# A transformer block on one core: a new ScalarE formula in the build's clock, fillers of zeros into open sums, earlier due times for side work

## The chip, the core and the metric

The kernel runs on one core of a Trainium2 chip. The core has a matrix engine (PE, with its weight loads shown apart as PEld), VectorE (DVE), ScalarE (ACT), GpSimd (POOL) and a queue that issues transfers (SP). The metric is device time in microseconds of one execution; times before are three runs, a profile is one execution of its own.

## The reference

One block with conditioning: a normalization scaled and shifted by vectors made from `c`, attention with 32 heads of 16, a residual, a second such normalization, a gated feed-forward network (FFN), a residual.

```python
h = _layernorm(x) * (1 + ca) + sa
x = x + ga * (softmax(q @ k.T * 16 ** -0.5) @ v) @ wo        # 2048 tokens, D = 512, H = 32
h = _layernorm(x) * (1 + cb) + sb
x = x + gb * ((gelu(h @ w_gate) * (h @ w_up)) @ w_down)      # F = 1792
```

## The kernel before

The program is written by a planner. `_Recorder` notes every instruction with what it reads and writes, works out the semaphores, and keeps a clock of its own, the build's clock: `cost` (L298 on) gives the duration of an ACT, DVE or POOL instruction, `model` the time of each engine. `probe` asks when an instruction could start. The order of instructions on each engine follows from these estimates, and the chip then runs that fixed order.

Attention runs over nine sets of query tokens: seven of 256 and two of 128 (sets 7 and 8). A unit is a set (some units take two sets together) with a group of four heads (`qd`); a round is a unit with a part of the keys; each round has four positions, and one position fills one PSUM bank of 512 scores. There are 2048 positions. Sets end at the positions 384, 512, 768, 1024, 1280, 1536, 1792, 1984 and 2048 (`ends`). The scores live in `ps_sc`, six banks in two halves of three. ScalarE takes a half with one exponential of three banks (128x1536), or of two (128x1024) where VectorE converts the third: it makes the bits of the exponential in one instruction, and after four banks (a group, "quad" in the code) three shifted copies (`shift_task`) that serve as parts of a better approximation. The products with V add into `ps_pv`, or for the second unit into the last bank of `ps_sc`; such a sum is open from the unit's first product to its last, then DVE copies it out (`unit_end`).

All other matrix work, the side work, goes through the one bank `ps_mi`: projections, output projection (`side_wo`), FFN (`side_ffn`), the transposes for it (`side_t`, `side_t2`). `plan` (L1277 on) lists it with a first position and a due position for each piece; from these comes a rate, and with every exponential the credit for side work grows by rate times positions, up to 4096. `next_side` and `advance` take the pieces in this order; while one holds the bank, `self.open` is true. In the loop of `stream` side work may run where the build's clock sees room; with a credit over 1536 it goes before the products with V. A new group for VectorE is begun, from position 1536 on, only while the credit is below CREDIT = 3500 (or where side work waits for the attention itself).

`short` sums the matmul columns of the last 3413 ns of the build's clock; below FILL = 3700 a filler may run: a product of the identity with a tile of `xs` into `ps_sc`, if the half is free but the exponential before it leaves time, or into `ps_mi`, if no piece holds it.

After the last position, `tail` finishes the sets 7 and 8: the gate and up products of set 7 that are not yet done, all those of set 8, and their down projections. Set 7's FFN can begin once its transposes (`t2T`) are done; these come in `before_last`, which takes turns with the FFN of set 6 for `ps_mi`.

Of the kernel before, what the change touches and what calls it, by code (L numbers as in the profile page):

```python
# [7 lines left out]
BF16 = mybir.dt.bfloat16  # L8
# [5 lines left out]
P = 128  # L14
# [9 lines left out]
VW = DH + 1  # L24
# [8 lines left out]
NSETS = len(SETS)  # L33
OCOL = (0, 256, 0, 256, 0, 256, 0, 256, 384)
BCOL = (0,) * (NSETS - 1) + (128,)
QJ = 4
QS = 4
MERGED = (((0, 1), (2, 3), (4, 5), (6,), (7,)), ((0, 1), (2, 3), (4,), (5,), (6,), (7,)))
CH = 3
SC = 2 * CH  # L40
# [49 lines left out]
class _Recorder:  # L90
# [21 lines left out]
    def sb(self, name, shape, dt):  # L112
        t = self.nc.alloc_sbuf_tensor(name, shape, dt)
        n = 1
        for s in shape[1:]:
            n *= s
        self.pitch[name] = n * mybir.dt.size(dt)
        self.kind[name] = "sb"
        return t
# [178 lines left out]
    def cost(self, eng, out, ins, kind):  # L298
        n = 1
        for _, k in (out if kind != "bn" else ins[0]).ap[1:]:  # L300
            n *= int(k)
        aps = [out] + list(ins)
        ps = any(self.kind.get(a.tensor.name) == "ps" for a in aps)
        small = all(mybir.dt.size(a.dtype) == 2 for a in aps)
        if eng == "act":
            return n * 0.833 + (51 if ps else 92)
        if eng == "pool":
            return n * 3.0 + 100
        f = 1
        if not ps:  # L310
            f = {("ts", True): 4, ("ts", False): 2, ("tt", True): 2}.get((kind, small), 1)
        elif small:
            f = 1.4
        return n * 1.042 / f + 68 + (95 if kind == "bn" else 0)
# [116 lines left out]
class _Kernel(_Recorder):  # L431
# [12 lines left out]
    def alloc(self):  # L444
        sb, ps = self.sb, self.ps
# [59 lines left out]
        self.rm4 = self.den[:, 0, 0:4]  # L505
        self.rm = sb("rm", [P, 2], FP32)
        self.ident = sb("ident", [P, P], BF16)
        self.ones = dreg[:, 10 * D:10 * D + P]
        self.half = dreg[:, 10 * D + P:10 * D + 2 * P]
        self.self32 = sb("self32", [P, P], FP32)  # L510
# [6 lines left out]
    def prologue(self):  # L517
        sp, act, pe, dve, pool = "sp", "act", "pe", "dve", "pool"
# [17 lines left out]

        half = self.half
        self.memset(dve, self.warm, 0.0)
        self.memset(dve, half[:, 0:2], 0.5)
        self.memset(dve, self.ones, 1.0)  # L540
        self.memset(dve, self.pv[:, :], 0.0)
# [546 lines left out]
    def side_ffn(self, gi, part=None):  # L1088

        q0, W = SETS[gi]  # L1090
        n = W // P
# [63 lines left out]
        def U(ci):  # L1155
# [4 lines left out]
            for b0 in range(0, m, kpb):  # L1160
# [5 lines left out]
                    self.task([lambda: self.tt("dve", prod[:, fcs[0]:fcs[0] + m, c0:c0 + W], w.rearrange("p (k n) -> p k n", k=m),  # L1166
                                               g.rearrange("p (k n) -> p k n", k=m), ALU.mult)], ("prod", gi, ci))
                yield END
        early = [part is not None]

        def near():
            if early[0] and ("osb", gi + 1, 5) in self.have:
                early[0] = False
                yield from self.near_end(gi + 1, 5, self.mi)
        nch = len(chunks)
# [101 lines left out]
    def plan(self, ends, nsplit, begin):  # L1277

        def at(i):
            return i * 2.5 if i < nsplit / 2.5 else nsplit + 3 * (i - nsplit / 2.5)  # L1280
        a = ends[0] + 33
        w = [(self.side_first, 0, at(30))]
        w.append((self.side_wo_load, at(30), at(30)))
        w.append((lambda: self.side_dc(1), at(30), at(51)))
        w.append((self.side_mod, at(50), at(59)))
        w.append((self.scale_wo, at(59), at(59)))
        b, c = begin[2] - 12, begin[3] - 12
        w.append((lambda: self.side_dc(2), at(59), b))
        w.append((lambda: self.side_dc(3), b, c))
        for g in range(1, 4):  # L1290
            w.append((lambda g=g: self.side_q_all(g), c + (a - c) * (g - 1) // 3, c + (a - c) * g // 3))
        n = ends[-1]
        m = NSETS - 2
        for k in range(m):
            s0 = ends[k] + 33
            e = ends[m] + 60
            if k < m - 1:
                e = max(ends[k + 1] + 30, ends[0] + 33 + (e - ends[0] - 33) * sum(SETS[k]) // SETS[m][0])
            w.append((lambda k=k: self.side_wo(k), s0, min(e, s0 + 15 * SETS[k][1] // P)))
            if k < m - 1:  # L1300
                w.append((lambda k=k: self.side_ffn(k), s0, e))
            else:
                w.append((lambda k=k: self.turns(self.before_last(m), self.side_ffn(k)), s0, e))
        k, s0 = NSETS - 2, ends[-2] - 16
        w.append((lambda: self.either(self.side_ffn(k, True), self.near_end(k + 1, 6, lambda: self.spare[2]), self.wo_last(k + 1), self.tail_rest(k, self.mi[:, :])), s0, n - 20))
        res = []
        for mk, s, e in w:
            self.dry = True
            tot = sum(y[0] for y in mk() if y is not None)
            self.dry = False  # L1310
            res.append([mk(), s, e, tot, None])
        return res
# [43 lines left out]
    def stream(self):  # L1356
# [9 lines left out]
        m = NSETS - 2  # L1366
        units = [((0, 1), qd, 0, 512) for qd in range(QJ)]
# [8 lines left out]
        ends = [0] * NSETS  # L1376
# [13 lines left out]
        for u in units[2:]:  # L1390
            n, kpb = NKT * u[3] // 512, 512 // u[3]
            plain = list(range(T0 // kpb))
            m = len(plain) * 2 // 3
# [111 lines left out]
        while cg <= group[units[-1]]:  # L1505
# [114 lines left out]
            if self.short(t) > 0 and not self.open and gap > 213 and self.probe(  # L1620
                    lambda: self.mm(self.mi[:, :], *filler)) <= t + 30:
                self.mm(self.mi[:, :], *filler)
                continue
            nxt = [x for x in [tq, ts] + [x[0] for x in tp] if x is not None and x > t + 30]
            if self.tasks:
                nxt.append(max(self.free["dve"], t + 100))
# [55 lines left out]
    def unit_end(self, u, acc):  # L1682
        sets, qd, q0, W = u
        b, lo, hi = self.osb_span(u)
        assert not self.blocked(u)
        self.copy("dve", self.osb[:, lo:hi], acc[:, 0:W])
        if sets[0] >= NSETS - 2 and len(sets) == 1 and qd >= (6 if sets[0] == NSETS - 2 else 5):
            self.done(("osb", sets[0], qd))
            return
        self.live[u] = (lo, hi)  # L1690
        two = W == 256 and sets[0] < NSETS - 2 or len(sets) > 1 and sets[0]
        if two and qd % 2 == 0:
            return
        us = [u]
        if two:
            us, lo, b = [(sets, qd - 1, q0, W), u], lo - W, b - 1
        L = hi - lo
        m = 4 * L // P
        o = 8 if BCOL[sets[0]] else 0
        sem = b + 4 * (o > 0)  # L1700
        late = EARLY if qd < 6 else (0, 0, 0)
        s2 = self.scr2[b, P * o:P * o + 4 * L]
        den, rden = self.den[:, b, o:o + m], self.rden[:, b, o:o + m]
        c = OCOL[sets[0]]
        steps = [
            ("sp", lambda: self.dma("sp", den, self.osb[DH:P:32, lo:hi].rearrange("j (a n) -> j a n", n=m), "db%d" % sem, late=late[0])),
            lambda: self.recip(rden, den),
            ("sp", lambda: self.dma("sp", s2.rearrange("(p n) -> p n", p=P), rden, "dc%d" % sem)),
            ]
        steps += [("sp", lambda j=j: self.dma(  # L1710
            "sp", self.rb[32 * j:32 * j + DH, lo:hi],
            s2[L * j:L * j + L].rearrange("(o n) -> o n", o=1).broadcast_to([DH, L]), "dd%d%d" % (sem, j), late=late[1]))
            for j in range(4)]

        def fin2():
            n = len(us)
            self.tt("dve", self.onorm[:, qd + 1 - n:qd + 1, c:c + W], self.osb[:, lo:hi].rearrange("p (a n) -> p a n", a=n),
                    self.rb[:, lo:hi].rearrange("p (a n) -> p a n", a=n), ALU.mult)
            if self.probing is None:
                for v in us:  # L1720
                    self.live.pop(v)
                for v in us:
                    for k in sets:
                        self.done(("half" if v[1] in odd else "onorm", k, v[1]))

        odd = [g[1] for g in self.merged(sets[0]) if len(g) == 2]

        def merge(j):
            self.dma("sp", self.onorm[32 * j + DH:32 * j + 2 * DH, 0:2 * len(odd):2, c:c + W], self.onorm[32 * j:32 * j + DH, 1:2 * len(odd):2, c:c + W],
                     "de%d" % j, late=late[2])  # L1730
            if self.probing is None and j == 3:
                for k in sets:
                    for x in odd:
                        self.done(("onorm", k, x))

        def free():
            return ("den", u) in self.have and all(
                ("wo", k) in self.have for k in range(sets[0]) if OCOL[k] < c + W and c < OCOL[k] + SETS[k][1])
        self.task(steps, ("den", u))
        self.task([fin2], ("norm", u), free)  # L1740
        if qd == odd[-1]:
            self.task([("sp", lambda j=j: merge(j)) for j in range(4)], None,
                      self.after([("half", k, x) for k in sets for x in odd] + [("onorm", k, x - 1) for k in sets for x in odd]))
# [220 lines left out]
```

## Time and profile before

| | us |
|---|---|
| median of three runs (827.96 to 829.52) | 828.34 |
| the profiled execution | 828.3 |
| its span, first to last instruction | 826.5 |
| mean granted clock of PE | 0.989 |

The page gives the busy time of each engine over the span. The chain of work that ended last is followed back from the last instruction to what released it. Groups are instructions of one line and form: busy time, mean duration, and idle time before them. Where instructions of an engine overlap, the mean duration of one is longer than the distance between two starts.

### The profile page before, as it was taken

How to read it: one execution, taken by the hardware profiler on the slowest of the kernel's cores; microseconds unless marked ns; L12 is line 12 of the kernel's file. 1: busy time of each engine (PE TensorE's matmuls, PEld its weight loads, DVE VectorE, ACT ScalarE, POOL GpSimd, SP SyncE). 2: the span in 40 equal slices, each digit the busy share in tenths (PEclk: the TensorE clock that was granted, in tenths of full speed). 3: DMA queues.
4: the chain of work that ended last, by engine and by line, in shares of the span. 5: the costliest groups of instructions: out<-in, count | busy, mean ns of one | idle time of the engine just before them, and what ended most of it. 6: DMA issues, size and time to landing. Idle time of an engine off the chain costs nothing.

```text
span 826.5 us, 37027 instructions
## 1 busy us (share of the span) xinstructions
PE 753.5 (91%) x17040; PEld 366.2 (44%) x17040; DVE 722.6 (87%) x1452; ACT 792.4 (96%) x746; POOL 4.5 (1%) x12
## 2 busy tenths in 40 slices
PE   8889899998989898999899989989899889988898
PEld 4333334333544444334444444344534443346557
DVE  7854878999999999999999799999988999979854
ACT  6999999999999999999999899999999999999982
POOL 2000000000000000000000000000000000000000
PEclk9989999999999999999999799999999999999999
DMA  9100000012451054103420243005423532200000
GB/s 299 53 12 13 10 9 11 10 27 59 136 146 33 16 161 121 40 10 110 125 86 16 78 130 97 25 22 164 110 68 107 178 93 66 72 10 11 18 12 13
DMA packets 94498, 57.35 MB, mean 69 GB/s; under 512 B 17030, under 2 KB 91911, under 8 KB 94343
## 3 DMA queue, kind: packets, MB, share of 16 engines
q1 hardware_dynamic: 93812, 54.47, 23.1%
q8 instruction: 133, 2.18, 1.1%
q10 hardware_dynamic: 530, 0.53, 0.2%
q14 instruction: 23, 0.18, 0.1%
HBM read 50.04 MB, written 2.35 MB: 63 GB/s over the span
## 4 chain that ended last, share of the span: by engine, by line
ACT 84%; PE 15%; DVE 1%; issue 1%
ACT E L338 81%; PE ps_sc L325 6%; PE ps_mi L325 5%; PE ps_pv L325 3%; ACT wreg L338 3%; PE ps_mi L329 0%; DVE mreg L350 0%; DVE xs L342 0%; DVE wreg L342 0%; DVE wreg L355 0%; PE ps_sc L329 0%; DVE wreg L350 0%; ACT hreg L338 0%; DVE osb L359 0%; DVE kT L359 0%
## 5 line engine op out<-in xcount | busy, mean ns | idle before, releaser
L338 ACT ACTIVATE E<-ps_sc 128x1024 bf16<-128x1024 f32 (+2 forms) x700 | 767.7, 1349 | 19.7 <-PE ps_sc L325 19.4
L325 PE MATMUL ps_sc<-qT,kT 32*128 32x256 bf16 (+3 forms) x2048 | 202.3, 275 | 26.7 <-ACT E L338 22.6
L325 PE MATMUL ps_sc<-qo,kT 32*128 32x256 bf16 (+2 forms) x2048 | 197.5, 274 | 27.1 <-ACT E L338 24.8
L325 PE MATMUL ps_pv<-E,vaug 128*17 128x256 bf16 (+2 forms) x3232 | 156.8, 275 | 1.0 <-DVE osb L359 0.7
L350 DVE TENSOR_SCALAR dreg<-ps_sc 128x512 uint16<-128x512 f32 x192 | 130.4, 685 | 13.9 <-PE ps_sc L325 13.2
L325 PE MATMUL ps_mi<-wreg,mreg 128*32 128x256 bf16 x2816 | 117.0, 277 | 4.2 <-DVE wreg L355 2.1
L325 PEld LDWEIGHTS ps_sc<-qT,kT 32*128 32x128 bf16 (+1 forms) x2048 | 62.1, 92 | 117.1 <-ACT E L338 101.9
L325 PEld LDWEIGHTS ps_sc<-qo,kT 32*128 32x128 bf16 x2048 | 59.9, 92 | 119.7 <-ACT E L338 111.6
L325 PEld LDWEIGHTS ps_pv<-E,vaug 128*17 128x17 bf16 x3232 | 60.5, 89 | 61.6 <-issue 40.8
L325 PEld LDWEIGHTS ps_mi<-wreg,mreg 128*32 128x32 bf16 x2816 | 64.7, 96 | 40.8 <-issue 25.5
L325 PE MATMUL ps_pv<-mreg,vs 128*17 128x256 bf16 (+2 forms) x1796 | 79.9, 269 | 2.1 <-issue 1.7
L350 DVE TENSOR_SCALAR mreg<-dreg 128x2048 uint16<-128x2048 uint16 x120 | 80.8, 682 | 1.0 <-PE ps_pv L325 0.8
L350 DVE TENSOR_SCALAR kq<-ps_sc 128x512 uint16<-128x512 f32 x96 | 65.2, 685 | 5.2 <-PE ps_sc L325 4.7
L350 DVE TENSOR_SCALAR mreg<-ps_sc 128x512 uint16<-128x512 f32 x96 | 65.2, 685 | 5.0 <-PE ps_sc L325 4.5
L325 PEld LDWEIGHTS ps_pv<-mreg,vs 128*17 128x17 bf16 x1796 | 40.0, 91 | 16.5 <-issue 6.5
L359 DVE CAST wreg<-ps_mi 128x512 bf16<-128x512 f32 x49 | 33.5, 684 | 5.2 <-PE ps_mi L325 4.2
L325 PE MATMUL ps_mi<-hreg,wreg 128*32 128x512 bf16 (+1 forms) x496 | 37.3, 384 | 0.5 <-DVE vaug L359 0.2
L355 DVE SCALAR_TENSOR_TENSOR wreg<-wreg,ps_mi 128x512 bf16<-128x512 bf16 x49 | 33.2, 678 | 1.9 <-ACT wreg L338 1.1
L342 DVE TENSOR_TENSOR wreg<-wreg 128x1024 bf16<-128x1024 bf16 (+1 forms) x56 | 34.3, 614 | 0.0
L350 DVE TENSOR_SCALAR mreg<-kq 128x2048 uint16<-128x2048 uint16 x48 | 32.1, 680 | 2.0 <-PE ps_pv L325 1.9
L350 DVE TENSOR_SCALAR mreg<-mreg 128x2048 uint16<-128x2048 uint16 x48 | 32.5, 677 | 0.1
L338 ACT ACTIVATE wreg<-wreg 128x1024 bf16<-128x1024 bf16 (+1 forms) x28 | 31.1, 1111 | 0.0
(171 smaller groups left out, 701.0 us busy)
## 6 DMA issues: line engine op xcount, KB each, us to landing
mreg<-in_B_w_up_dram SPq DMA_DIRECT2D x46, 256.0 KB, 3.0
mreg<-in_B_w_gate_dram SPq DMA_DIRECT2D x42, 256.0 KB, 3.1
dreg<-in_B_w_down_dram SPq DMA_DIRECT2D x18, 256.0 KB, 3.4
rb<-scr_rec SPq DMA_DIRECT2D x120, 32.0 KB, 2.3
mreg<-in_B_w_down_dram SPq DMA_DIRECT2D x12, 256.0 KB, 3.7
ereg<-in_B_w_down_dram SPq DMA_DIRECT2D x12, 256.0 KB, 3.5
mreg<-in_w_mod_dram SPq DMA_DIRECT2D x1, 2048.0 KB, 12.9
out_dram<-xs SPq DMA_DIRECT2D x15, 128.0 KB, 1.7
```

What stands on the lines that cost most here:

```text
L325: return self.rec("pe", lambda e: e.matmul(out, lhsT, rhs, start=start, stop=stop, tile_position=tp), [lhsT, rhs], [out], cost=(n, int(rhs ...
L338: return self.rec("act", lambda e: e.activation(out, in_, func, scale=scale, **kw), rd, wr, cost=self.cost("act", out, [in_], "act"))
L342: return self.rec(eng, lambda e: e.tensor_tensor(out, a, b, op), [a, b], [out], cost=self.cost(eng, out, [a, b], "tt"))
L350: return self.rec(eng, lambda e: e.tensor_scalar(out, a, s1, s2, **kw), rd, [out], cost=self.cost(eng, out, [a], "ts") + 60 * (len(rd) - 1 ...
L355: return self.rec("dve", lambda e: e.scalar_tensor_tensor(out, a, s, b, op0=op0, op1=op1), rd, [out], cost=self.cost("dve", out, [a, b], " ...
L359: return self.rec(eng, lambda e: e.tensor_copy(out, in_), [in_], [out], cost=self.cost(eng, out, [in_], "ts"))
```

## The change

```diff
+LONE = max(5, QS)
...
         if eng == "act":
-            return n * 0.833 + (51 if ps else 92)
+            return n * 0.8333 + (64 if ps else 82)
...
+        self.zero = sb("zero", [P, P], BF16)
...
         self.memset(dve, self.warm, 0.0)
+        self.memset(pool, self.zero[:, :], 0.0)
...
-        early = [part is not None]
+        early = [part is not None and LONE == 5]
...
-            if early[0] and ("osb", gi + 1, 5) in self.have:
+            if early[0] and ("osb", gi + 1, LONE) in self.have:
...
             s0 = ends[k] + 33
-            e = ends[m] + 60
+            e = ends[m] - (20)
             if k < m - 1:
                 e = max(ends[k + 1] + 30, ends[0] + 33 + (e - ends[0] - 33) * sum(SETS[k]) // SETS[m][0])
...
                 self.mm(self.mi[:, :], *filler)
                 continue
+            if self.short(t) > 0 and pos < nseq:
+                u = next((u for u in units if group[u] == cg and u in begun and left[u] > 0), None)
+                if u is not None and gap > u[3] / 2.4:
+                    def nought():
+                        for j in range(4):
+                            self.mm(acc_of(u)[32 * j:32 * j + VW, 0:u[3]], self.zero[:, 0:VW], filler[1][:, 0:u[3]], start=False, stop=False, tp=(0, 32 * j))
+                    if self.probe(nought) <= t + 30:
+                        nought()
+                        continue
...
-        if sets[0] >= NSETS - 2 and len(sets) == 1 and qd >= (6 if sets[0] == NSETS - 2 else 5):
+        if sets[0] >= NSETS - 2 and len(sets) == 1 and qd >= (6 if sets[0] == NSETS - 2 else LONE):
...
-        if two and qd % 2 == 0:
+        if two and qd % 2 == 0 and (sets, qd + 1, q0, W) in self.units:
             return
         us = [u]
-        if two:
+        if two and qd % 2:
             us, lo, b = [(sets, qd - 1, q0, W), u], lo - W, b - 1
```

Four edits act on the program. The estimate of a ScalarE instruction becomes 0.8333 ns per element plus 64 ns from PSUM (it was 0.833 and 51) or 82 ns otherwise (it was 92). A tile of zeros is set up on POOL. Where `short` calls for a filler and the older places for one did not serve, four matmuls with the zeros as stationary operand add nothing to the sum of a unit that is begun and not ended, if the next scores are further away than one such matmul takes. And the due position from which the FFN's times are worked out moves from `ends[7] + 60` = 2044 to `ends[7] - 20` = 1964. LONE has the value 5, with QS = 4.

## The prediction

> **What bounds the kernel now.** I read the page first: the span, the busy times, the chain of work that ended last, the costliest group.
>
> ```profile
> span 826.5 us, 37027 instructions
> ...
> ACT 84%; PE 15%; DVE 1%; issue 1%
> ...
> L338 ACT ACTIVATE E<-ps_sc 128x1024 bf16<-128x1024 f32 (+2 forms) x700 | 767.7, 1349 | 19.7 <-PE ps_sc L325 19.4
> ```
>
> ScalarE's exponentials set the end: 767.7 us in this one group, and 84% of the chain. So a microsecond is won where ScalarE waits, where it gets less to do, or behind its last exponential. The table by stretches says where it waits (busy time of PE, weight loads, DVE, ACT, POOL with counts, then granted clock, DMA share, GB/s).
>
> ```profile
> 43.80:47.30 3.50, 2.27 (x23) 0.89 (x23) 2.53 (x8) 3.50 (x4) 0.00 (x0) 1.00 0.01 2
> 47.30:54.20 6.90, 6.83 (x49) 2.18 (x49) 1.80 (x4) 5.57 (x6) 0.00 (x0) 0.51 0.01 2
> 453.60:457.00 3.40, 2.41 (x46) 0.89 (x42) 1.92 (x7) 3.40 (x4) 0.00 (x0) 0.99 0.00 0
> 457.00:467.10 10.10, 10.04 (x132) 3.70 (x128) 6.01 (x12) 8.39 (x8) 0.00 (x0) 0.50 0.18 52
> 467.10:505.00 37.90, 34.75 (x890) 18.52 (x886) 36.72 (x66) 37.13 (x36) 0.00 (x0) 1.00 0.45 129
> 505.00:700.00 195.00, 178.58 (x4081) 84.52 (x4083) 185.76 (x353) 195.00 (x186) 0.00 (x0) 1.00 0.33 92
> 700.00:757.00 57.00, 51.37 (x1292) 26.34 (x1289) 50.05 (x99) 57.00 (x52) 0.00 (x0) 1.00 0.12 33
> 757.00:777.00 20.00, 17.20 (x674) 12.85 (x676) 17.32 (x39) 18.94 (x17) 0.00 (x0) 1.00 0.10 17
> 800.00:826.50 26.50, 23.30 (x337) 19.57 (x325) 13.01 (x38) 7.24 (x14) 0.00 (x0) 0.98 0.05 15
> ```
>
> From 505 to 757 us ScalarE never pauses. At 47.3 and at 457.0 the granted clock falls to half for 6.9 and 10.1 us: there PE is always busy and ScalarE idles 6.90 - 5.57 = 1.33 and 10.10 - 8.39 = 1.71 us, with 37.90 - 37.13 = 0.77 us more just after. Ahead of each fall PE had little to do: 2.27 of 3.50 us and 2.41 of 3.40. And after 800, with the exponentials over, 26.5 us of tail belong to PE (23.3 busy).
>
> **The zero matmuls.** PE around the first fall and ahead of the second (start, length, operation, count, idle before):
>
> ```profile
> 45.76 0.62 PE L329 MATMUL ps_mi<-ident,dreg 128*128 128x128 bf16 x8
> 46.31 0.39 PE L325 MATMUL ps_sc<-qT,kT 32*128 32x512 bf16 x2
> 47.37 0.61 PE L325 MATMUL ps_sc<-qT,kT 32*128 32x512 bf16 x3 [0.67 <-ACT E L338]
> ```
>
> ```profile
> 454.12 0.40 PE L325 MATMUL ps_pv<-E,vaug 128*17 128x256 bf16 x8
> 455.14 0.10 PEld L325 LDWEIGHTS ps_sc<-xs,ident 128*32 128x32 bf16 x4 [0.91 <-ACT E L338]
> 455.14 0.40 PE L325 MATMUL ps_sc<-xs,ident 128*32 128x512 bf16 x4 [0.62 <-ACT E L338]
> ```
>
> Both times transposes (L329) held ps_mi open, so the old filler had no bank; PE stood 0.67 and 0.62 us. The new branch goes there: four matmuls of zeros into the open sum. A stationary operand of 17 columns over 256 moving columns takes 0.40 us in a group of 8, by the first row of the second fence, pipeline end included, so some 0.11 us for four; over 512 columns some 0.21. The branch fires only where the build's clock sees a longer gap, so the time is PE's idle time. PE's idle time in the two thin stretches, 1.23 and 0.99 us, holds five long or nine short ones at most. I take the whole of 1.33 + 1.71 + 0.77 = 3.8 us as won; the bounds are -3.8 and 0 (the clock falls as before).
>
> Do zeros count as work? The kernel's own start answers: its warm-up matmuls multiply a tile that was set to zero.
>
> ```profile
> 1.25 2.31 PE L325 MATMUL ps_mi<-dreg 128*128 128x512 bf16 x5 [1.25 <-DVE dreg L366]
> ...
> 7.79 1.02 PE L325 MATMUL ps_mi<-dreg 128*128 128x512 bf16 x4
> ```
>
> Five take 2.31 us at first and four take 1.02 us later, 0.46 and 0.26 us each, and between them PE ran mostly such zeros. So zeros seem to raise the clock.
>
> The Trainium skill, "TensorE: Matmul & The Clock Gate", section "HAM oscillation — how this bites in real kernels", gives as the rule that PE must not idle for more than some 3.4 us. By that rule these pauses, all under 1 us, were harmless, the clock fell for another reason, and the zeros would win nothing: the sum would lack its 3.8 us. The trace differs, since both falls follow 3.4 us of thin PE work without any long pause; I go by the trace.
>
> What the fillers cost: they use another tiling of the array than the scores, and wait for nothing that is not long done. If one ends late, the next scores are some 0.1 us late (the four's own time), which ScalarE's running exponential covers; without this cover each costs 0.1. I allow +0.2 us in all, bounds 0 and +2 (twenty uncovered).
>
> **ScalarE in the build's clock.** Between two tanh the exponentials stand back to back:
>
> ```profile
> 54.34 164.49 ACT L338 ACTIVATE E<-ps_sc 128x1536 bf16<-128x1536 f32 x150
> 218.58 1.18 ACT L338 ACTIVATE wreg<-wreg 128x1024 bf16<-128x1024 bf16 x1
> ```
>
> ```profile
> L338 ACT ACTIVATE E<-ps_sc 128x1536 bf16<-128x1536 f32 x63 | 93.6, 1587 | 0.1
> L338 ACT ACTIVATE E<-ps_sc 128x1024 bf16<-128x1024 f32 x87 | 89.2, 1177 | 0.0
> ```
>
> 164.24 us hold 63 wide and 87 narrow ones. With 512 elements more at 0.833 ns (427 ns), the narrow one takes (164.24 - 63 x 0.427) / 150 = 0.916 us and the wide one 1.342. The old formula says 0.904 and 1.331, the new one 0.917 and 1.344. So the old clock ran 13 ns fast in each exponential, 9 us over 692 of two and three banks, and the new one is true. Nothing on the chip gets shorter by it; the written order changes everywhere. With ScalarE 9 us longer in the build's clock, VectorE gets 9 us in which it can take exponentials over. VectorE takes a group of four scores in seven instructions, and these start 0.6 us apart where they are dense:
>
> ```profile
> 689.56 0.69 DVE L350 TENSOR_SCALAR dreg<-ps_sc 128x512 uint16<-128x512 f32 x1
> 690.16 0.68 DVE L350 TENSOR_SCALAR mreg<-mreg 128x2048 uint16<-128x2048 uint16 x1
> 690.76 0.68 DVE L350 TENSOR_SCALAR dreg<-ps_sc 128x512 uint16<-128x512 f32 x1
> ```
>
> That is 4.2 us a group: room for two more, and each spares ScalarE four banks of 0.427 us, 1.71 us. Bounds: -3.4 us (two) and 0 (VectorE, 185.76 of 195.00 us busy from 505 to 700, has no real room). I take half a group, -0.9.
>
> **The earlier due times.** The last term of the plan moves from position 2044 to 1964. For the feed-forward networks (FFN) of sets 0 to 4 that is 11 to 36 positions of 2048, and set 5 keeps its time (another term of the maximum holds it). Set 6 must now be through in 139 positions in place of 219. Before, its work reached the last exponentials: the normalized rows of set 7, their transposes, and the tail's gate and up products.
>
> ```profile
> 792.38 0.41 DVE L350 TENSOR_SCALAR hreg<-xs,mv,rstd 128x512 bf16<-128x512 bf16 x1
> ```
>
> ```profile
> 800.07 0.28 PE L329 MATMUL ps_mi<-ident,hreg 128*128 128x128 bf16 x2
> ...
> 805.05 1.06 PE L325 MATMUL ps_sc<-wreg,mreg 128*128 128x128 bf16 x16
> 805.94 1.06 PE L325 MATMUL ps_sc<-wreg,qT 128*128 128x128 bf16 x16
> ```
>
> Set 7 was normalized at 792.8, but its transposes came at 800.07, once set 6 had left ps_mi. So all 112 gate and up matmuls of set 7 ran in the tail, 16 in 0.89 us (805.05 to 805.94). If set 6 ends some 5 us earlier, one or two blocks of 32 run beside the last exponentials. Two blocks are 4 x 0.89 = 3.6 us off the tail: one bound. The other: the moved work overfills PE between 700 and 757, where 57.00 - 51.37 = 5.6 us are free, and ScalarE idles there as it does from 757 to 777, 1.06 of 20 us: 57 x 5.3% = +3.0 us. I take -1.3, nearer to the gain, since ps_mi with its single bank holds the work back before PE is full.
>
> **At nothing:** LONE is 5 as QS is 4, and every even unit has its odd partner, so these edits leave the program as it is. The zero tile's memset goes ahead of the identity's on POOL, about as long as this one:
>
> ```profile
> 0.80 0.20 POOL L366 MEMSET ident<- 128x128 bf16 x1 [0.29 <-POOLq L1949]
> ```
>
> The identity is first read by transposes after the warm-up matmuls of 7.79 us, far later; uncovered it would cost 0.2.
>
> **Sum** against the profiled execution's 828.3 us (span 826.5 plus 1.8 around it; the median is 828.34, so no correction): -3.8 + 0.2 - 0.9 - 1.3 = -5.8, so 822.5 us.
>
> **Rivals.**
>
> *The clock falls all the same* (the zeros stand too late, or the new order opens another thin stretch). For it: the old filler did not prevent either fall. Against: it had no bank there. Then 828.3 + 0.2 - 0.9 - 1.3 = 826.3.
>
> *PE overfull.* The FFN of set 6 starves ScalarE by 3.0 us. For it: the 5.3% from 757 to 777. Against: the planner lets side work in only where its clock sees room. 822.5 + 3.0 = 825.5.
>
> *Slower: VectorE's share is refused.* From position 1536 on, no new group goes to VectorE while the credit for side work is 3500 or more; the due time at 1964 drives the credit to its cap of 4096 sooner and keeps it there. From 697 to 800 us VectorE converted 42 banks, 10.5 groups:
>
> ```profile
> L350 DVE TENSOR_SCALAR dreg<-ps_sc 128x512 uint16<-128x512 f32 x18 | 12.2, 684 | 2.0 <-PE ps_sc L325 1.9
> ...
> L350 DVE TENSOR_SCALAR mreg<-ps_sc 128x512 uint16<-128x512 f32 x12 | 8.2, 686 | 0.7 <-PE ps_sc L325 0.6
> L350 DVE TENSOR_SCALAR kq<-ps_sc 128x512 uint16<-128x512 f32 x12 | 8.1, 685 | 0.4 <-PE ps_sc L325 0.4
> ```
>
> Each lost group gives ScalarE 1.71 us; four (6.8) outweigh the whole gain. With five lost and only the clock's 3.8 won: 828.3 + 8.5 - 3.8 = 833.0. Against: a block of side work takes 2048 off the credit and opens the door for a moment.
>
> **How the numbers follow.** Forecast 0.50; the clock falls all the same 0.16; PE overfull 0.14; share refused 0.20. The bounds of the three gains together give 828.3 - 3.8 - 3.4 - 3.6 = 817.5, the low end, taken as 817. The high end, 830, takes in both milder rivals and the refused share of up to three groups (828.3 - 3.8 + 5.1 = 829.6); about 0.17 stays outside. A change under 0.2%, 1.7 us, can't be told from none: same is 826.6 to 830.0. Faster: 0.50 + 0.10 of the first rival + 0.13 of the second = 0.73. Same: the rest of these two, 0.07, and 0.04 of the third, 0.11. Slower: 0.16.
>
> **What would show it.** Right: no stretch with the clock at 0.5 after the start; a group of matmuls with a zero tile into ps_pv or ps_sc, some tens of them, most near the former falls; transposes of set 7 before the last exponential and fewer than 224 gate and up matmuls of 128 columns behind it; 384 or more VectorE conversions. Wrong: a clock of 0.5 anywhere (first rival), ScalarE idle by some us between 700 and 786 (second), clearly under 384 conversions, missing late (third).

## The result, and the profile after

| | before | after |
|---|---|---|
| median of 17 runs, us | 827.83 | 824.23 |
| lowest and highest, us | 825.85 and 833.12 | 821.37 and 827.72 |
| ratio, 95% interval | | 0.9953 (0.9939 to 0.9966) |
| the profiled execution, us (its span) | 828.3 (826.5) | 827.72 (826.0) |
| its mean granted clock | 0.989 | 0.992 |

The changed kernel is faster by 3.6 us, and the interval keeps clear of one. The profiled execution of after is the longest of its 17, so its trace can't be set against that of before as a gain of 3.6 us: it is 0.6 us shorter. The page of after (span; busy time of each engine; granted clock in 40 slices, in tenths; the chain of waits by engine; the costliest group):

```profile
span 826.0 us, 37305 instructions
...
PE 754.6 (91%) x17162; PEld 368.5 (45%) x17166; DVE 732.1 (89%) x1473; ACT 787.7 (95%) x746; POOL 4.6 (1%) x13
...
PEclk9979999999999999999999999999999999999999
...
ACT 76%; PE 18%; DVE 4%; DMA 1%; issue 1%; SPq 0%; DVEq 0%
...
L339 ACT ACTIVATE E<-ps_sc 128x1024 bf16<-128x1024 f32 (+2 forms) x700 | 762.7, 1311 | 23.7 <-PE ps_sc L326 23.3
```

The group of exponentials has lost 767.7 - 762.7 = 5.0 us of work, and the idle time ahead of it has grown by 23.7 - 19.7 = 4.0 us. The clock line still has a 7. That group by its forms says which work went (count, busy time and mean, idle time before), in before and then in after:

```profile
L338 ACT ACTIVATE E<-ps_sc 128x1024 bf16<-128x1024 f32 x412 | 421.3, 1192 | 5.5 <-PE ps_sc L325 5.4
L338 ACT ACTIVATE E<-ps_sc 128x1536 bf16<-128x1536 f32 x280 | 417.3, 1602 | 2.6 <-PE ps_sc L325 2.3
...
L338 ACT ACTIVATE E<-ps_sc 128x512 bf16<-128x512 f32 x6 | 3.6, 597 | 9.3 <-PE ps_sc L325 9.3
```

```profile
L339 ACT ACTIVATE E<-ps_sc 128x1024 bf16<-128x1024 f32 x424 | 427.6, 1158 | 7.7 <-PE ps_sc L326 7.4
L339 ACT ACTIVATE E<-ps_sc 128x1536 bf16<-128x1536 f32 x268 | 395.8, 1576 | 3.0 <-PE ps_sc L326 2.9
...
L339 ACT ACTIVATE E<-ps_sc 128x512 bf16<-128x512 f32 x6 | 3.6, 597 | 10.7 <-PE ps_sc L326 10.7
```

Twelve wide exponentials became narrow ones: VectorE took over 12 banks, three groups of four. At the prediction's 0.427 us a bank that is 5.1 us, the whole of the work that went. The idle time came back in two places: between the exponentials (7.7 + 3.0 against 5.5 + 2.6, so 2.6 us more) and before the six short ones of 512 columns (1.4 us more). Those six, and two of 256 columns in the same group of 700, are no exponentials: they are the gate's activations in the tail, behind the table load, and write a tile of the same name. VectorE's conversions agree (the page, count and busy time), first before, then after:

```profile
L350 DVE TENSOR_SCALAR dreg<-ps_sc 128x512 uint16<-128x512 f32 x192 | 130.4, 685 | 13.9 <-PE ps_sc L325 13.2
...
L350 DVE TENSOR_SCALAR mreg<-ps_sc 128x512 uint16<-128x512 f32 x96 | 65.2, 685 | 5.0 <-PE ps_sc L325 4.5
```

```profile
L351 DVE TENSOR_SCALAR dreg<-ps_sc 128x512 uint16<-128x512 f32 x200 | 136.0, 688 | 8.2 <-PE ps_sc L326 7.0
...
L351 DVE TENSOR_SCALAR mreg<-ps_sc 128x512 uint16<-128x512 f32 x100 | 68.0, 687 | 4.4 <-PE ps_sc L326 3.7
L351 DVE TENSOR_SCALAR kq<-ps_sc 128x512 uint16<-128x512 f32 x96 | 65.3, 688 | 3.7 <-PE ps_sc L326 3.2
```

With kq's 96 in both, 384 conversions became 396. The zero matmuls are there, eleven groups of four, the first at 22.2 us and the last at 731.3 (PE's groups by form):

```profile
L326 PE MATMUL ps_pv<-xs,zero 128*17 128x256 bf16 x32 | 1.9, 292 | 0.0
...
L326 PE MATMUL ps_pv<-xs,zero 128*17 128x512 bf16 x12 | 1.2, 379 | 0.0
```

But the clock fell all the same. The table by stretches of after (length, busy time of PE, weight loads, DVE, ACT, POOL with counts, granted clock, DMA share, GB/s), and PE ahead of the first fall:

```profile
36.80:40.20 3.40, 2.73 (x35) 1.29 (x31) 2.65 (x8) 3.40 (x4) 0.00 (x0) 1.00 0.00 0
40.20:51.30 11.10, 10.37 (x124) 3.93 (x122) 5.90 (x20) 7.72 (x7) 0.00 (x0) 0.54 0.01 2
440.00:467.00 27.00, 23.19 (x556) 11.48 (x552) 25.43 (x57) 26.77 (x26) 0.00 (x0) 1.00 0.20 58
...
620.80:624.20 3.40, 2.43 (x57) 0.86 (x52) 3.37 (x7) 3.40 (x5) 0.00 (x0) 1.00 0.77 215
624.20:627.70 3.50, 3.50 (x44) 1.09 (x44) 2.88 (x5) 2.71 (x3) 0.00 (x0) 0.55 0.11 30
```

```profile
38.83 0.39 PE L326 MATMUL ps_sc<-E,vaug 128*17 128x512 bf16 x4
39.05 0.39 PE L326 MATMUL ps_pv<-xs,zero 128*17 128x512 bf16 x4
39.37 0.62 PE L330 MATMUL ps_mi<-ident,dreg 128*128 128x128 bf16 x8
...
40.77 0.56 PE L326 MATMUL ps_sc<-qo,kT 32*128 32x512 bf16 x3 [0.46 <-ACT E L339]
```

A group of zeros stands at 39.05, in the thin stretch itself, and the clock falls 1.8 us later, at 40.9 (the second row begins a little ahead of the fall and ends a little behind it). ScalarE idles 11.10 - 7.72 = 3.38 us there and 3.50 - 2.71 = 0.79 us in the fall at 624: 4.2 us, where the prediction counted 3.8 for the falls of before. The fall at 457 is gone, though no zeros stand between 440 and 475. So in this execution the falls cost no less than those of before; the order won 5 us of exponentials and lost most of it in waits and in the tail.

### The profile page after: what moved, and what is told of

Its sections match the earlier page's. It is cut to its first block, busy times and chain, and to the rows that moved or that the text cites. A ratio compares the mean times of both kernels' runs of the same rounds, so it can differ in the third digit from the quotient of the medians.

```text
span 826.0 us, 37305 instructions
## 1 busy us (share of the span) xinstructions
PE 754.6 (91%) x17162; PEld 368.5 (45%) x17166; DVE 732.1 (89%) x1473; ACT 787.7 (95%) x746; POOL 4.6 (1%) x13
## 4 chain that ended last, share of the span: by engine, by line
ACT 76%; PE 18%; DVE 4%; DMA 1%; issue 1%; SPq 0%; DVEq 0%
ACT E L339 73%; PE ps_mi L326 7%; PE ps_sc L326 7%; PE ps_pv L326 3%; ACT wreg L339 2%; DVE mreg L351 1%; DMA mreg<-in_B_w_up_dram 1%; DVE dreg L351 0%; DVE wreg L356 0%; DVE kq L351 0%; DVE kT L360 0%; DVE wreg L360 0%; DVE sq L351 0%; DVE wreg L343 0%; DVE osb L360 0%
## 5 line engine op out<-in xcount | busy, mean ns | idle before, releaser
L339 ACT ACTIVATE E<-ps_sc 128x1024 bf16<-128x1024 f32 (+2 forms) x700 | 762.7, 1311 | 23.7 <-PE ps_sc L326 23.3
L326 PE MATMUL ps_sc<-qo,kT 32*128 32x256 bf16 (+2 forms) x2048 | 199.7, 273 | 22.1 <-ACT E L339 19.3
L351 DVE TENSOR_SCALAR dreg<-ps_sc 128x512 uint16<-128x512 f32 x200 | 136.0, 688 | 8.2 <-PE ps_sc L326 7.0
L326 PE MATMUL ps_mi<-wreg,mreg 128*32 128x256 bf16 x2816 | 109.2, 275 | 7.2 <-DVE wreg L360 2.0
L326 PE MATMUL ps_pv<-mreg,vs 128*17 128x256 bf16 (+2 forms) x1852 | 83.3, 269 | 1.2 <-issue 0.6
L351 DVE TENSOR_SCALAR mreg<-dreg 128x2048 uint16<-128x2048 uint16 x125 | 83.8, 686 | 0.3 <-PE ps_pv L326 0.3
L351 DVE TENSOR_SCALAR mreg<-ps_sc 128x512 uint16<-128x512 f32 x100 | 68.0, 687 | 4.4 <-PE ps_sc L326 3.7
L326 PEld LDWEIGHTS ps_pv<-mreg,vs 128*17 128x17 bf16 x1852 | 40.8, 90 | 16.3 <-issue 6.5
L351 DVE TENSOR_SCALAR mreg<-mreg 128x2048 uint16<-128x2048 uint16 x50 | 34.2, 683 | 0.0
L360 DVE COPY osb<-ps_pv 128x256 f32<-128x256 f32 (+2 forms) x63 | 26.1, 414 | 5.9 <-PE ps_pv L326 5.3
```

Of the source, the lines that this page charges most:

```text
L326: return self.rec("pe", lambda e: e.matmul(out, lhsT, rhs, start=start, stop=stop, tile_position=tp), [lhsT, rhs], [out], cost=(n, int(rhs ...
L339: return self.rec("act", lambda e: e.activation(out, in_, func, scale=scale, **kw), rd, wr, cost=self.cost("act", out, [in_], "act"))
L351: return self.rec(eng, lambda e: e.tensor_scalar(out, a, s1, s2, **kw), rd, [out], cost=self.cost(eng, out, [a], "ts") + 60 * (len(rd) - 1 ...
L360: return self.rec(eng, lambda e: e.tensor_copy(out, in_), [in_], [out], cost=self.cost(eng, out, [in_], "ts"))
```

## The experiments

The theory: the falls of the clock cost ScalarE time, and the zeros prevent them. The rival that the profile of after suggests: each edit deals another order of all the work, and the order decides, with or without zeros on PE. All four edits were taken apart. Falls are told from 10 us on, by stretches of 1 us with a granted clock under 0.9. The ratios are estimates over all runs of a kernel, with an interval, and not quotients of the medians.

**The changed kernel again, the zeros planned but not issued, data in place of zeros, and the branch never taken.** These four ran on one chip, with before at 826.52 us. The edits, in this order (the first run is the changed kernel itself):

```diff
+        if self.ghost:
+            self.model(_Op(eng, stream, seq, fn), max(at, self.free[eng]), cost)
+            return None
...
+                        self.ghost = True
                         nought()
+                        self.ghost = False
```

```diff
-                            self.mm(acc_of(u)[32 * j:32 * j + VW, 0:u[3]], self.zero[:, 0:VW], filler[1][:, 0:u[3]], start=False, stop=False, tp=(0, 32 * j))
+                            self.mm(acc_of(u)[32 * j:32 * j + VW, 0:u[3]], filler[1][:, 0:VW], filler[1][:, 0:u[3]], start=False, stop=False, tp=(0, 32 * j))
```

```diff
-            if self.short(t) > 0 and pos < nseq:
+            if self.short(t) > 0 and pos < 0:
```

> The changed kernel again, as the anchor for the three beside it: 0.995 of the kernel before, some 824 us. Theory A (the times scatter because the clock falls in some executions and not in others): runs with a mean granted clock of 1.0 lie near 822, those below 0.995 near 825 or above. Rival (the scatter has another cause): no relation between a run's clock and its time.

> The same order of instructions as the changed kernel on every engine; only the eleven groups of four zero matmuls are counted in the build's clock and not issued. Theory A (the zeros hold the clock, 3.8 us as predicted): the clock falls more often, mean clock 0.98 to 0.99, time 2 to 4 us above the changed kernel. Rival B (the eleven groups are too few and the gain comes from the new order): within 1 us of the changed kernel, the same mean clock.

> The changed kernel with 17 columns of x in the place of the zeros, so that these fillers add products of x to the open sums (the outputs differ by that). Same order, same number of matmuls. Theory A (zeros count as work like any matmul): time and mean clock as the changed kernel, within 1 us and 0.003. Rival C (a multiplier fed with zeros counts less): a higher clock and 1 to 3 us less.

> The changed kernel without the branch for zeros; the build's clock and the due times are the new ones. Theory A (zeros won most): 3 to 4 us above the changed kernel, about 827.5. Rival B (formula and due times won it by the new order): 823 to 825.

| kernel | median us (runs) | ratio to before, 95% | mean clock |
|---|---|---|---|
| changed kernel again | 822.97 (7) | 0.9961 (0.9947 to 0.9974) | 0.9966 |
| zeros planned, not issued | 823.03 (5) | 0.9965 (0.9952 to 0.9978) | 0.9960 |
| data in place of zeros | 822.06 (5) | 0.9949 (0.9937 to 0.9961) | 0.9974 |
| branch never taken | 834.92 (6) | 1.0108 (1.0079 to 1.0136) | 0.9890 |

The kernel without a single zero matmul on PE, but in the same order (the two traces have the same instructions in the same order on every engine, the zeros aside), is as fast as the changed one: 823.03 against 822.97. So to issue them is worth nothing in this order that these runs could see. Without the branch the kernel is 12 us slower, more than either expectation allowed. Neither this kernel nor the one with the zeros planned only has zeros on PE, so the 12 us between them are the order's: the branch moves the build's clock on by four matmuls at eleven places, and everything after each place is planned anew. By the slope worked out below, some 3 of the 12 us come through its lower mean clock. Data in place of zeros can't be told from zeros; but neither can no filler at all, so that run can't say whether zeros count as work. Within the seven runs of the changed kernel the time goes with the clock, as expected: 821.38 to 822.39 us at 0.998 and more, 824.79 and 825.63 at 0.994. The rival holds for the whole change.

The same program also has its falls elsewhere in another execution. The changed kernel again, by stretches:

```profile
617.90:621.30 3.40, 2.32 (x44) 0.68 (x40) 2.88 (x6) 3.40 (x5) 0.00 (x0) 1.00 0.48 104
621.30:624.70 3.40, 3.35 (x38) 1.03 (x38) 3.09 (x5) 2.44 (x3) 0.00 (x0) 0.53 0.61 171
```

It fell at 20, 621 and 768 us here, and not at 40. The kernel without the branch, its costliest group and the longest of its eight falls, is what an order looks like that keeps PE badly fed (this execution, 841.72 us, is the slowest of its six):

```profile
L339 ACT ACTIVATE E<-ps_sc 128x1024 bf16<-128x1024 f32 (+2 forms) x700 | 765.9, 1296 | 32.7 <-PE ps_sc L326 31.9
```

```profile
371.80:375.20 3.40, 2.57 (x57) 1.03 (x54) 2.89 (x8) 3.40 (x5) 0.00 (x0) 1.00 0.02 5
375.20:385.60 10.40, 10.21 (x132) 3.79 (x130) 8.45 (x17) 8.38 (x9) 0.00 (x0) 0.52 0.07 15
```

Its exponentials are 1.8 us shorter than those of before (767.7), but ScalarE waits 32.7 us ahead of them, 13.0 more than in before.

**Each part alone, and the change without each part.** With the run above this makes every combination of formula, zeros and due position. The edits to the changed kernel are these lines, set back to those of before or not; where the zeros are out, the branch and its tile are out:

```diff
-            return n * 0.8333 + (64 if ps else 82)
+            return n * 0.833 + (51 if ps else 92)
...
-            e = ends[m] - (20)
+            e = ends[m] + 60
```

> The kernel before with the new ScalarE formula alone. As predicted: VectorE takes over half a group to two groups more (386 to 392 conversions), 0.9 us less, bounds 0 and 3.4. Rival B (the formula carries the whole gain): 3 to 4 us less, three groups or more.

> The kernel before with the zero tile and the branch for zeros alone. As predicted: neither of the two falls of the clock, 3 to 4 us less, mean clock 0.998 or more. Rival B: at most 1 us less, a fall somewhere in most executions.

> The kernel before with the due position at 1964 alone. As predicted: 1.3 us less, the transposes of set 7 before the last exponential, fewer than 224 gate and up matmuls of 128 columns in the tail. Rival D (ps_mi holds the side work of set 6 back, the due time changes nothing there): all 224 in the tail, time within 1 us of before. Rival E (refused groups): under 384 conversions, 2 to 7 us more.

> The changed kernel with the due position back at 2044. Rival D: within 1 us of the changed kernel, 0.995 of before. As predicted: 1.3 us above the changed kernel.

> The changed kernel with the old ScalarE formula: the zeros and the due position at 1964 alone, the last cell of the eight combinations. If the parts simply added up, by the runs so far: zeros alone -3.3 us, due position alone +1.1, together 2 us less than before. Theory F (each edit deals a new order, and what it brings depends on the others): off this sum by 2 us or more, either way.

Each ratio is to the runs of before on the same chip (826.54 us for the first four rows, 825.56 for the fifth); groups are VectorE's conversions divided by four, 96 in before.

| parts in the kernel | median us (runs) | ratio, 95% | groups | mean clock |
|---|---|---|---|---|
| formula | 827.44 (12) | 0.9998 (0.9979 to 1.0017) | 98 | 0.9953 |
| zeros | 823.40 (7) | 0.9953 (0.9934 to 0.9972) | 97 | 0.9986 |
| due position | 828.14 (12) | 1.0014 (1.0000 to 1.0027) | 98 | 0.9948 |
| formula and zeros | 827.08 (12) | 1.0004 (0.9984 to 1.0023) | 99 | 0.9960 |
| zeros and due position | 825.85 (12) | 1.0000 (0.9986 to 1.0014) | 97 | 0.9972 |

The parts do not add up. The formula alone is worth nothing in time although VectorE takes two groups more; the due position alone takes two groups more as well, and loses, if anything. Both together lose 1.1%, and with the zeros' branch they win 0.4 to 0.5%, no more than the branch alone. Take one of the two away from the full change, and the gain is gone: zeros and due position by themselves would add up to 0.9967, and measure 1.0000. Averaged over the four kernels with a part and the four without it (before with its 1, the changed kernel with the 0.9961 of its second measurement), the branch gives 0.9980 against 1.0030, the formula 1.0018 against 0.9992, and the due position 1.0021 against 0.9989: only the branch helps on the average, and each mean hides a spread of up to 1.5%.

**Zeros on PE alone, more zeros, and a neighbour of the due position.** The first, with before's formula and due position, keeps before's own order on every engine and issues eleven groups of zeros that the build's clock does not count; the second raises FILL in the changed kernel, so that `short` asks for more; the third moves the due position by 20.

```diff
+        if self.quiet:
+            op.t1 = 0.0
+            return op
...
-                    if self.probe(nought) <= t + 30:
+                    if t >= self.after_zero and self.probe(nought) <= t + 30:
+                        self.quiet = True
                         nought()
-                        continue
+                        self.quiet = False
+                        self.after_zero = t + u[3] / 2.4
```

```diff
-FILL = 3700
+FILL = 4300
```

```diff
-            e = ends[m] - (20)
+            e = ends[m] - (0)
```

> The kernel before with its own order kept on every engine; eleven groups of four zero matmuls are issued where the branch's condition holds, and not counted in the build's clock. Theory A (the zeros as such hold the clock): mean clock 0.998, 1 to 3 us less than before. Theory F (the zeros work by the new order alone): within 0.7 us of before and the same mean clock, 0.995.

> The changed kernel with FILL = 4300 in the place of 3700, so that fillers of all kinds are planned earlier: 29 groups of zeros in the place of 11. If the falls of the clock follow from what the plan counts: mean clock 0.999 or more, and 1 to 2 us less than the changed kernel by the slope of 3.5 us for 0.01 of mean clock. Theory F: the clock as said, the time anywhere within 4 us of the changed kernel.

> The changed kernel with the due position at 1984 in the place of 1964, a quarter of the way back to 2044. As predicted (an earlier due time ends set 6 earlier): between the changed kernel and the one with 2044, 824 to 826 us. Theory F (a new order without a trend): outside of these, by 2 us or more.

| kernel | median us (runs) | ratio to before at 825.56, 95% | mean clock |
|---|---|---|---|
| zeros on PE in before's order | 823.79 (12) | 0.9975 (0.9961 to 0.9990) | 0.9975 |
| FILL 4300 in the changed kernel | 821.37 (8) | 0.9948 (0.9929 to 0.9967) | 0.9984 |
| due position 1984 in the changed kernel | 829.06 (12) | 1.0035 (1.0022 to 1.0048) | 0.9946 |

In before's order the zeros do win, 1.8 us (the traces of the two have the same order on every engine but for the zeros). The mean clock is 0.9975 against 0.9959; single runs scatter by 0.003, so that rise is not clear of noise. FILL 4300 has the lowest median of all, and each of its eight runs had a clock of 0.998 or more; its interval overlaps that of the changed kernel, so it is not shown to be better, and since it was not run with its zeros planned and not issued, zeros and order stay mixed in it. Its page and its groups of zeros, 32 of them where 29 were expected:

```profile
L339 ACT ACTIVATE E<-ps_sc 128x1024 bf16<-128x1024 f32 (+2 forms) x700 | 763.3, 1328 | 16.3 <-PE ps_sc L326 16.3
```

```profile
L326 PE MATMUL ps_pv<-xs,zero 128*17 128x256 bf16 x92 | 5.3, 274 | 0.0
...
L326 PE MATMUL ps_pv<-xs,zero 128*17 128x512 bf16 x36 | 3.5, 382 | 0.0
```

ScalarE waits 16.3 us ahead of this group. The kernel with the zeros planned only, whose profile has the same clock of 0.998, waits 19.8 us. So the 5.3 + 3.5 = 8.8 us of zeros that PE has to do cost nothing that shows. A due position 20 away from the changed kernel's makes it 0.35% slower than before: its value is not a setting with a smooth effect.

**Where the order's gain goes.** Two profiled executions have a clock of 0.998 and one short fall each: zeros in before's order, and the changed order without zeros. So they show the two orders with nearly the same clock; they are single executions on two chips. ScalarE about the end of the long exponentials, first in before's order, then in the changed one (start, length, operation, count, idle before):

```profile
796.44 1.28 ACT L344 ACT_TABLE_LOAD   x1
...
801.31 0.60 ACT L344 ACTIVATE E<-ps_sc 128x512 bf16<-128x512 f32 x1 [3.38 <-PE ps_sc L331]
```

```profile
791.98 1.28 ACT L343 ACT_TABLE_LOAD   x1
...
798.95 0.60 ACT L343 ACTIVATE E<-ps_sc 128x512 bf16<-128x512 f32 x1 [5.46 <-PE ps_sc L330]
```

The table load comes right behind the last long exponential: 4.5 us earlier in the changed order. Then ScalarE waits 5.46 us in place of 3.38. Of the spans, 822.6 and 820.2, the part from there on is 26.2 and 28.2 us, so some 2 of the 4.5 us are given back in the tail. The end of the profiled execution of after shows where (ScalarE, then PE):

```profile
798.21 1.28 ACT L339 ACT_TABLE_LOAD   x1
```

```profile
792.51 0.28 PE L330 MATMUL ps_mi<-ident,hreg 128*128 128x128 bf16 x2
...
795.00 1.25 PE L326 MATMUL ps_mi<-xs,hreg 128*32 128x512 bf16 x20
...
797.91 0.86 PE L326 MATMUL ps_mi<-xs,hreg 128*32 128x512 bf16 x12
...
800.17 0.59 PE L326 MATMUL ps_mi<-hreg 128*128 128x512 bf16 x2
...
802.96 0.78 PE L326 MATMUL ps_sc<-wreg,qT 128*128 128x128 bf16 x11
```

Set 7's transposes moved ahead (792.51, where before had them at 800.07), but into the middle of set 6's down projections: the second (xs and hreg into ps_mi) holds the one bank until 800.8, and the chain of work that ended last runs through these products. The gate and up products start 4.75 us behind the table load at 798.21. Before started them 3.39 us behind its table load (ScalarE, then PE):

```profile
800.12 1.28 ACT L338 ACT_TABLE_LOAD   x1
```

```profile
803.51 0.78 PE L325 MATMUL ps_sc<-wreg,qT 128*128 128x128 bf16 x11
```

## Why the prediction was right or wrong

**The direction, the range and the bound were right.** 824.2 us lies in the range, ScalarE still sets the end, and the gain is real. The sum was too large: 5.8 us against 3.6. That the three terms together came out as a gain is in part luck: the formula alone (0.9998) and the due position alone (1.0014) win nothing, the two together lose 1.1%, and the gain of the whole hangs on the order that it happened to deal.

**The zeros, -3.8 us: mis-sized, and in the changed order not theirs.** Three steps went into it. That a fall costs what was read holds: over the 73 runs of before beside the experiments, the time goes with the mean clock at 3.9 us per 0.01 (correlation -0.70; 4.2 and 4.0 on the two chips with some 30 runs, 0.8 on the one with 12), and at that slope the profiled execution, 0.011 below full clock, lost 4.3 us where 3.8 were read. But that execution was no typical one. The mean clock of the 73 runs is 0.9955, so full clock is worth 0.45 x 3.9 = 1.75 us, not 3.8; the 26 runs at 0.998 or more averaged 825.5 and the others 826.9. A term read off one execution should have been asked whether it recurs in the next.

The second step, that the zeros prevent falls, holds in part. In before's order the clock is 0.0016 higher with them, which the slope makes 0.6 us, against 1.8 measured. In the changed order nothing is left of it (823.03 and 822.97).

The third step, that a thin stretch leads to a fall, was drawn from the two thin stretches ahead of the two falls and did not ask for thin stretches without one. Cut into 445 windows of 3.4 us, 1.7 us apart, from 24 us on, the trace of before has 74 with PE busy 2.8 us or less at full clock, that of after 66, and FILL 4300 55, with two, two and no falls in that part of the trace. Eleven groups of zeros can't fill these. Nor does the old filler's missing bank explain the falls: the prediction's own row at 455.14, the identity with `xs` into `ps_sc`, is an old filler at work 1.8 us ahead of the second fall, so it had a bank there. And transposes stood ahead of both falls in before, but none stood in the 3.4 us ahead of the one at 624 in after, nor ahead of those at 20, 621 and 768 in the second execution.

In the 3.4 us ahead of each of the changed kernel's falls PE idles 1.1 us at most, all pauses together (3.40 - 2.32 in the row at 617.9), and the falls come at 40 and 624 us in one execution, at 20, 621 and 768 in the other. The rule that the prediction weighed, of the Trainium skill, "TensorE: Matmul & The Clock Gate", section "HAM oscillation — how this bites in real kernels", asks only that PE not pause for more than some 3.4 us; the falls differ from it. On the same page of the Trainium skill the section "A second HAM failure mode: psum-queue depth-cycling" says that frequent short idle times between groups of matmuls make the clock go back and forth, and the section "What's actually happening" that the window in which activity is counted runs freely, so that the count of slow matmuls at a start differs from run to run. These falls agree with both: no pause is long, and where they lie follows a grid that starts elsewhere from execution to execution. In the clock records of all 14 traces, each fall begins a whole number of times 3.413 us behind the clock's first rise: 12 and 132 times in before, 10 and 181 in after, 4, 180 and 223 in its second execution, where the first rise itself came at 7.09 in place of 6.72 us.

On that grid the thin stretch does better than in the windows above. Count each matmul from its start for its columns alone, at 0.435 ns a column (16 of 128 columns start 0.89 us apart), since PE's busy time holds the ends of the pipeline too. Then the 14 emptiest of 3,213 stretches at full clock up to 800 us, in the 14 traces, are all followed by a fall, and all 26 falls follow one of the emptiest 89 (1.70 us of columns or less, where half of the stretches have some 2.5 or more). So the work in one such stretch seems to decide, and a thin spell that straddles two stretches seems to pass. This is a count over traces and not an experiment; but the build's clock, which sums the last 3.413 us at any moment, can't know where the grid will lie.

**The formula, -0.9 us: the step likely right, its size and its yield wrong.** For the exponentials from PSUM the new formula is the true one, and VectorE did take more: two groups more with the formula alone, three in the change, where half a group was taken. The due position alone brought two as well, so a new order does it too; over the eight kernels, the four with the formula have 98.5 groups on the average and the four without it 97.0. Their price, 1.71 us a group, holds in the page (5.0 us for three). But alone these groups brought nothing (0.9998): 767.7 - 764.0 = 3.7 us of exponentials less, and ScalarE's idle time ahead of them 22.6 in place of 19.7. The prediction priced what ScalarE is spared and not how PE must keep up when the exponentials come sooner.

**The due position, -1.3 us: failed.** One of its signs came as foretold, transposes of set 7 at 792.5, before the last long exponential. But it is no sign of this edit: with formula and zeros and the old due position (PE, then ScalarE) they stand 5.4 us ahead of the table load as well.

```profile
789.77 0.28 PE L330 MATMUL ps_mi<-ident,hreg 128*128 128x128 bf16 x2 [0.35 <-DVE xs L343]
```

```profile
795.14 1.28 ACT L339 ACT_TABLE_LOAD   x1
```

And the other sign failed: all 224 gate and up matmuls of 128 columns are still behind the last long exponential, with the due position alone too. PE's groups by form, from 798.2 us to the end of after:

```profile
L326 PE MATMUL ps_sc<-wreg,qT 128*128 128x128 bf16 x96 | 7.0, 219 | 0.2
L326 PE MATMUL ps_sc<-wreg,mreg 128*128 128x128 bf16 x64 | 4.2, 219 | 0.0
L326 PE MATMUL ps_sc<-wreg,dreg 128*128 128x128 bf16 x48 | 3.4, 219 | 0.0
...
L326 PE MATMUL ps_sc<-wreg,hreg 128*128 128x128 bf16 x16 | 1.2, 219 | 0.0
```

ps_mi's one bank had gone back to set 6. The prediction saw that bank as a brake on the loss and did not count it as a brake on the gain. Alone the edit measures 1.0014. In the company of the other two it is worth some 3.5 us (a ratio of 1.0004 without it, 0.9961 with it, on two chips), while the position 20 later spoils the kernel, with set 7's transposes at 801.96, behind the table load at 799.73. So an earlier due position did not by itself mean that set 6 was done sooner: that is the order dealt anew.

**The rivals.** *The clock falls all the same* came true, in the profiled execution (827.72, forecast 826.3) and on the mean (0.9966 after). *PE overfull* did not: ScalarE never pauses from 700 to 757 us and idles 1.26 us from 757 to 777, where it idled 1.06 in before (after, by stretches). *The share refused* did not: 396 conversions. What was missing is the rival that won: the edits change the plan, and the plan moved the time by anything from 0.5% less to 1.1% more, whatever the edit was for.

```profile
700.00:757.00 57.00, 52.20 (x1323) 26.06 (x1318) 54.03 (x107) 57.00 (x54) 0.00 (x0) 1.00 0.13 33
757.00:777.00 20.00, 17.27 (x643) 12.35 (x634) 17.96 (x38) 18.74 (x19) 0.00 (x0) 1.00 0.11 18
```

**What makes up the 3.6 us,** as far as shown: the order, at nearly the same clock, 822.6 - 820.2 = 2.4 us, a rough figure from two single executions on two chips, the first of them with zeros; the clock, 0.9966 against 0.9955, at the slope 0.4 us. The other 0.8 us are not assigned. Also open: why zeros in before's order win more than their clock explains (at 0.998 and more, 823.4 against 825.0 us), and why the due position wins beside formula and branch together (0.9961 against 1.0004) and loses in every other company (1.0014 alone, 1.0108 against 0.9998 with the formula, 1.0000 against 0.9953 with the branch).

## What to carry to other kernels

Where a program is planned by a model of the chip, an edit to the model or to one rule of it is a new plan: measure it against the same edit with its instructions left out (planned, not issued), and against its neighbours in value, before the edit is given the credit. A loss read from one execution is worth what it costs in the mean of many: here the profiled one had more than twice the usual loss of clock. And work taken off the bounding engine counts only as far as the engine that feeds it, and the tail behind it, can follow.

## What was not expected of the hardware

Falls of the granted clock to half last one, two or three times 3.413 us: 6.8 and 10.2 us in before, 10.2 and 3.4 in after, 10.2 the longest in the kernel without the branch, 3.4 in each of the three of the changed kernel's second execution. They begin on a grid of the same step, counted from the clock's first rise. Each fall followed a stretch of 3.4 us with PE busy for 1.5 to 2.8 us, yet dozens of stretches as thin by that measure had none behind them; by the time of their columns alone the stretches that end in a fall stand out far better. The same program falls at other places from execution to execution. Whether a matmul with a stationary operand of zeros counts for less than one with data is open: 822.06 us with data and 822.97 with zeros have overlapping intervals, but so has 823.03 with neither.
